# Queries and keys as seven tokens per partition, loads on one queue, and FFN pairs of one weight, in a fused attention and FFN kernel

## Chip, cores and metric

The kernel runs on one core of one Trainium2 chip. The metric is the device time in microseconds (us). Before the change it is 394.41 us, the median of three runs (393.36 to 396.3). A profiled execution is a single run; its span, 390.3 us before the change, is about 1.7 us shorter than the time of that same run, 392.04 us.

## The reference, cut to what matters

```python
q, k, v: (8 batches, 12 heads, 448 tokens, 64)
def rmsnorm(x, g):
    return x / np.sqrt(np.mean(x * x, axis=-1, keepdims=True) + 1e-06) * g
scores = np.matmul(rmsnorm(q, g_q), rmsnorm(k, g_k).transpose(0, 1, 3, 2)) / 8
attn = softmax(scores)
x = (attn @ v).transpose(0, 2, 1, 3).reshape(3584, 768)
a, b = x @ w1, x @ w2                  # 768 -> 1024 each
out = (a * b @ w3) @ w_out             # 1024 -> 1024 -> 768
```

## The kernel before

Four heads of a batch are a "quad": three quads a batch, 24 in all. A quad is loaded (its queries and keys as fp32), squared on ScalarE, summed on VectorE, scaled by the inverse norm, transposed, multiplied to scores on TensorE, exponentiated on ScalarE (seven exponentials of 128x896), and multiplied by the values. The first five quads are transposed on TensorE, the rest by DMA. Since nothing stands between `@ w3` and `@ w_out`, the kernel computes the "weight product" `w34 = w3 @ w_out` once, at the start, and the FFN then is two products a batch: FFN1 (w1 and w2, then a * b) and FFN2 (w34). TensorE interleaves all this. A model inside the program (durations of each instruction, which load lands when) fixes the order of instructions on every engine when the program is built.

The parts that the change touches:

```python
J = 4; NF = 3; REST = 64               # 448 = 64 * 4 + 64 * 3 tokens
qk_bufs = [const.tile([NP, 2, HQ, J, D], FP, ...) for z in range(3)]    # padded to 512
POOL_ORDER = "o0 o1 w0 w1 v0 w2 w3 w4 w5 v1 w6 w7 a0 b0 v2 a1 b1 a2 b2 v3".split()
GATES = {1: "w0", 2: "w5", 3: "b0", 4: "a2"}   # quad i is asked for when that weight has landed
# o = w_out, w = w3, a = w1, b = w2, v = values of a quad
# ...
def load_qk(i, which, z, eng, h0=0, n=HQ):      # z: the half with 4 or with 3 tokens a partition
    p0, p1, nj, t0, t1 = halves[z]
    return eng.dma_start(
        out=t_sb[p0:p1, h0 : h0 + n, 0:nj, :].rearrange("p h j d -> p h (j d)"),
        in_=src[b, HQ*m + h0 : HQ*m + h0 + n, t0:t1].rearrange("h (p j) d -> p h (j d)", j=nj))
# ...
for t_sb in qk_bufs:                            # the padding is set to zero
    nc.vector.memset(t_sb[REST:NP, :, :, NF, :], 0.0)
# quad 0 loaded in eight pieces, then
nc.gpsimd.tensor_copy(out=gate, in_=qk_bufs[0][:, 0, 2, 0, 0:1])   # weights wait for quad 0
# ...
def ffn1_pair(b, fi):                           # one tile of w1 beside one of w2
    nc.scalar.copy(out=hold["a"], in_=ps_all[:, z, 0:S])           # 128x448
    nc.vector.tensor_tensor(out=abT[bp][:, fi, ...], in0=ps_all[:, z + 1, 0:S],
                            in1=hold["a"], op=MULT)
    # both weights and all of x must have landed
```

Of the kernel before, what the change touches and what calls it, by code (L numbers as in the profile page):

```python
# [24 lines left out]
LAG = {"ACT": 0.11, "DVE": 0.09, "SP": 0.0, "POOL": 0.0}  # L25


class Job:



    def __init__(self, engine, took, key, emit, needs=(), done=None, moves=None):
        self.engine, self.took, self.key = engine, took, key
        self.emit, self.needs, self.done, self.moves = emit, needs, done, moves
# [5 lines left out]
class Planner:  # L40
# [3 lines left out]
    def __init__(self):  # L44
        self.free = {e: 0.0 for e in ("ACT", "DVE", "SP", "POOL", "PE")}
        self.jobs = []
        self.lanes = {"SP": [], "POOL": []}
        self.moving = {"SP": [], "POOL": []}
        self.now = 0.0
        self.landed = {"SP": [], "POOL": []}  # L50
        self.moved_to = 0.0
# [3 lines left out]

    def advance(self, t):

        while self.moved_to < t:
            heads = [
                q[0] for q in self.moving.values() if q and q[0][0] <= self.moved_to  # L60
            ]
# [5 lines left out]
            if not heads:  # L67
# [4 lines left out]
                + [x[1] * len(heads) for x in heads]  # L72
                + [z - self.moved_to for z in starts]
            )
            for x in heads:
                x[1] -= step / len(heads)
            self.moved_to += step
            for q in self.moving.values():
                if q and q[0][1] <= 1e-9:
                    q[0][2](self.moved_to + 0.7)  # L80
                    q.pop(0)

    def next_move(self):
        heads = [q[0] for q in self.moving.values() if q and q[0][0] <= self.moved_to]
        starts = [q[0][0] for q in self.moving.values() if q and q[0][0] > self.moved_to]
        return min(
            [self.moved_to + x[1] * len(heads) for x in heads] + starts, default=INF
        )

    def commit(self, job, start):  # L90
        end = start + job.took
        self.free[job.engine] = end
        end += LAG[job.engine]
        self.jobs.remove(job)
        job.emit()
        if job.moves is not None:
            entry = [end + 1.0, job.moves, None]
            ticket = [INF]
            self.landed[job.engine].append(ticket)

            def landed(t, job=job, ticket=ticket):
                ticket[0] = t
                if job.done:
                    job.done(t)

            entry[2] = landed
            self.moving[job.engine].append(entry)
        elif job.done:
            job.done(end)

# [4 lines left out]
    def run(self, pe_step, finished):  # L115

        stuck = 0
        while not finished() or self.jobs:
            best = None
            for e in ("ACT", "DVE", "SP", "POOL"):  # L120
                mine = []
                for job in self.jobs:
                    if job.engine != e:
# [4 lines left out]
                    if ready < INF:  # L128
                        mine.append((max(ready, self.free[e], self.now), job.key, job))
# [6 lines left out]
                if best is None or start < best[0]:  # L136
                    best = (start, job)
# [14 lines left out]
            if best and best[0] <= self.next_move():  # L152
                self.now = max(self.now, best[0])
                self.commit(best[1], best[0])
# [9 lines left out]
def kernel(  # L164
# [16 lines left out]
    NP = 128  # L181
    J = -(-S // NP)
    NF = S // NP
    REST = S - NF * NP
    SPLIT = REST * J
# [18 lines left out]
    ffn_pool = ctx.enter_context(tc.tile_pool(name="ffn", bufs=3))  # L204
# [6 lines left out]
    WARM = 16  # L211
    POOL_ORDER = (
        "o0 o1 w0 w1 v0 w2 w3 w4 w5 v1 w6 w7 a0 b0 v2 a1 b1 a2 b2 v3".split()
    )
    GATES = {1: "w0", 2: "w5", 3: "b0", 4: "a2"}
# [14 lines left out]
    gate = const.tile([NP, 1], FP, name="gate")  # L230
    eps_t = const.tile([NP, 1], FP, name="eps_t")
    qk_bufs = [
        const.tile([NP, 2, HQ, J, D], FP, name="qk_sb" + str(z)) for z in range(3)
# [5 lines left out]
    halves = ((0, REST, J, 0, SPLIT), (REST, NP, NF, SPLIT, S))  # L239
# [18 lines left out]
    w_at = {"w3": [INF] * CF, "w3T": [INF] * CF, "w_out": [], "w1": [], "w2": []}  # L258
# [5 lines left out]
    sent, sent_at = {}, {}  # L264
# [9 lines left out]



    def load_qk(i, which, z, eng, h0=0, n=HQ):
        b, m = divmod(i, NQB)
        t_sb = qk_bufs[i % 3][:, which]
        src = (q, k)[which]  # L280
        p0, p1, nj, t0, t1 = halves[z]
        return eng.dma_start(  # L282
            out=t_sb[p0:p1, h0 : h0 + n, 0:nj, :].rearrange("p h j d -> p h (j d)"),
            in_=src[b, HQ * m + h0 : HQ * m + h0 + n, t0:t1].rearrange(
                "h (p j) d -> p h (j d)", j=nj
            ),
        )

    def gated(i, load):
        if i in GATES:  # L290
            tc.add_manual_dep(
                load.ins, sent[GATES[i]].ins.name, SYNC_DEP, reason="DMA engines first"
            )

    def plan_load_qk(i):
        for which in range(2):
            for z in range(2):
                def done(t, which=which):
                    parts = st[i].setdefault(("in", which), [])
                    parts.append(t)  # L300
                    if len(parts) == 2:
                        landed[i]["qk"[which]] = max(parts)

                add(
                    "SP", 0.62, QUAD * i - 30 + which, 
                    lambda which=which, z=z: gated(
                        i, load_qk(i, which, z, nc.sync)
                    ),
                    needs=[
                        lambda: qk_free[i % 3],  # L310
                        lambda: sent_at.get(GATES[i], INF) if i in GATES else 0.0,
                    ],
                    done=done,
                    moves=0.9,
                )

    def v_parts(i):
        b, m = divmod(i, NQB)
        v_sb = v_bufs[i % 4]
        src = v[b, HQ * m : HQ * (m + 1)]  # L320
        lo = src[:, 0:SPLIT].rearrange("h (p j) d -> p h j d", j=J)
        hi = src[:, SPLIT:S].rearrange("h (p j) d -> p h j d", j=NF)
        return (
            (v_sb[0:REST, 0:2], lo[:, 0:2]),
            (v_sb[0:REST, 2:4, 0:NF], lo[:, 2:4, 0:NF]),
            (v_sb[REST:NP, :, 0:NF], hi),
            (v_sb[REST:NP, 2:4, NF], lo[:, 2:4, NF]),
        )

    def load_v(i, z):  # L330
        dst, part = v_parts(i)[z]
        if z < 3:
            dst = dst.rearrange("p h j d -> p h (j d)")
            part = part.rearrange("p h j d -> p h (j d)")
        nc.gpsimd.dma_start(out=dst, in_=part)  # L335

    def plan_load_v(i, key):
# [7 lines left out]
        for z in range(4):  # L345
# [3 lines left out]
                moves=(0.48, 0.39, 0.78, 0.2)[z],  # L349
# [22 lines left out]
    def plan_prep(i):  # L372
# [3 lines left out]
        sq_at, red_at = [[], []], [INF, INF]  # L376
        src = qk_bufs[i % 3]
        got = lambda w: lambda: landed[i]["qk"[w]]

        def sq(pr, parts):  # L380
            hs = slice(2 * pr, 2 * pr + 2)
            if ("sq", pr) not in s:
                s["sq", pr] = prep_pool.tile([NP, 2, 2, J, D], FP, tag="sq", name="sq")
            for t in parts:
                nc.scalar.activation(  # L385
                    out=s["sq", pr][:, t], in_=src[:, t, hs], func=AF.Square
                )

        def red(pr, parts):
            hs = slice(2 * pr, 2 * pr + 2)  # L390
            if "ssq" not in s:
                s["ssq"] = prep_pool.tile([NP, 2, HQ, J], FP, tag="ssq", name="ssq")
            nc.vector.tensor_reduce(  # L393
                out=s["ssq"][:, parts, hs, :], in_=s["sq", pr][:, parts], axis=AX, op=ADD
            )

        def alpha(h0, h1):
            if "alpha" not in s:
                s["lnv"] = prep_pool.tile([NP, 2, HQ, J], FP, tag="lnv", name="lnv")
                s["alpha"] = prep_pool.tile([NP, 2, HQ, J], FP, tag="alpha", name="al")  # L400
            lnv = s["lnv"][:, :, h0:h1]
            nc.scalar.activation(
                out=lnv, in_=s["ssq"][:, :, h0:h1], func=AF.Ln, bias=eps_t
            )
            nc.scalar.activation(  # L405
                out=s["alpha"][:, :, h0:h1], in_=lnv, func=AF.Exp, scale=-0.5
            )

        def scale(pr, parts, with_g):
            hs = slice(2 * pr, 2 * pr + 2)  # L410
            if "qkT" not in s:
                s["qkT"] = qkT_pool.tile(
                    [128, 2, 2, J * NP], BF, tag="qkT", name="qkT"
                )
            if ("qks", pr) not in s:
                s["qks", pr] = prep_pool.tile(
                    [NP, 2, J, 2, D], BF, tag="qks", name="qks"
                )
            qks = s["qks", pr]
            for t in parts:  # L420
                nc.vector.tensor_tensor(  # L421
                    out=qks[:, t].transpose([0, 2, 1, 3]),
                    in0=src[:, t, hs],
                    in1=s["alpha"][:, t, hs].unsqueeze(3).broadcast_to([NP, 2, J, D]),
                    op=MULT,
                )
            if with_g:
                nc.vector.tensor_tensor(
                    out=qks[:, 0],
                    in0=qks[:, 0],  # L430
                    in1=g_b.unsqueeze(1).unsqueeze(1).broadcast_to([NP, J, 2, D]),
                    op=MULT,
# [696 lines left out]
```

## Time and profile before

| | before |
|---|---|
| median of the timed runs | 394.41 us |
| span of the profiled run | 390.3 us |
| TensorE, ScalarE, VectorE, GpSimd busy | 94, 67, 60, 17% |
| FFN starts (first w1 pass) | 72.4 us |
| attention ends on TensorE | 298.7 us |
| mean granted TensorE clock | 0.980 |

The prediction shows the page, the chain, the stretches and the groups. One finer cut matters for what follows. This is the table of stretches, with the columns time, busy time of PE, PEld, DVE, ACT and POOL with instruction counts, granted clock, DMA share and GB/s:

```profile
12.00:20.00 8.00, 5.21 (x45) 2.39 (x46) 2.13 (x5) 5.14 (x7) 2.07 (x5) 0.71 1.15 210
20.00:72.40 52.40, 45.41 (x835) 28.51 (x835) 28.53 (x44) 28.96 (x48) 15.69 (x27) 0.94 1.00 200
```

The reader should see that TensorE is busy for only 5.21 of the 8 us from 12 to 20 us, and at a clock of 0.71.

In all that follows, "lost" is the time of a stretch less the counted work of TensorE in it: passes of 448 columns at 0.189 us, of 384 columns at 0.162 us, transposes at 0.067 us. The first two come from the chain, as the prediction works out; the last is the program's own figure (the chain of after has 0.50 us for seven, 0.071 each). PE's busy time is more than that work: over the whole run before has 365.3 us of it, and 336 us of work by the prediction's count. Up to the FFN's start before loses 11.7 us (0 to 12), 5.5 (12 to 20) and 14.2 (20 to 72.4), 31.4 together.

### The profile page before, as it was taken

Reading aid. Unit: us, or ns where it says so; the run is one execution under the profiler, and the core shown is the slowest. Engines: PE = TensorE matmul, PEld = TensorE weight load, DVE = VectorE, ACT = ScalarE, POOL = GpSimd, SP = SyncE. Lnnn points to the kernel's source line nnn. Section 1 sums busy time; section 2 is a strip of 40 time slices with the busy share of each in tenths; the row PEclk is TensorE's granted clock in tenths of the full one; section 3 lists DMA queues with packets and bytes.
Section 4 is the critical chain, followed back from the end, with each engine's and each line's share of the span. In section 5 each row is a group of like instructions: output and inputs, shape, how many; then the busy total and the mean of one; then the engine's idle time right before and its main releaser. Section 6 shows DMA issues by size and latency. Waiting matters only on the chain.

```text
span 390.3 us, 16420 instructions
## 1 busy us (share of the span) xinstructions
PE 365.3 (94%) x7361; PEld 234.5 (60%) x7361; DVE 234.9 (60%) x366; ACT 262.0 (67%) x435; POOL 68.2 (17%) x119
## 2 busy tenths in 40 slices
PE   6587996999889999999999999999999999999994
PEld 2255653555555556856566565655656778778763
DVE  5425656379786895986879778878633223323232
ACT  4515768685999999999999899999973121120210
POOL 2452231340212122222221321220000000000000
PEclk9689999899999999999999999999999999999999
DMA  4999994935999999999999999995411302302105
GB/s 97 197 223 238 219 232 89 215 40 110 167 245 179 203 180 207 195 218 163 198 161 202 202 178 188 212 236 106 64 24 47 79 2 65 104 3 81 45 12 154
DMA packets 90986, 56.38 MB, mean 144 GB/s; under 512 B 56740, under 2 KB 85668, under 8 KB 90916
## 3 DMA queue, kind: packets, MB, share of 16 engines
q1 hardware_dynamic: 70208, 42.35, 52.9%
q0 software_dynamic: 19968, 12.33, 23.8%
q8 instruction: 57, 0.93, 1.0%
q10 hardware_dynamic: 740, 0.66, 0.7%
q14 instruction: 13, 0.11, 0.1%
HBM read 46.66 MB, written 11.01 MB: 148 GB/s over the span
## 4 chain that ended last, share of the span: by engine, by line
PE 77%; DMA 11%; ACT 6%; issue 2%; SPq 1%; DVE 1%; POOL 1%; DVEq 0%; POOLq 0%; ACTq 0%
PE ps_all L709 56%; PE ps_all L624 13%; PE ps_all L577 8%; DMA qk_sb<-in_q_dram 7%; ACT P L597 3%; DMA w3s<-in_moe_w_dram 3%; DMA w2s<-in_moe_w_dram 2%; ACT sq L385 1%; PE ps_all L912 1%; SPq L282 1%; ACT Pr L597 1%; POOL w_outs L365 0%; DVE o_sb L834 0%; ACT w34s L760 0%; ACT r L639 0%
## 5 line engine op out<-in xcount | busy, mean ns | idle before, releaser
L709 PE MATMUL ps_all<-xT,w2s 64*64 64x448 bf16 x1536 | 161.6, 350 | 1.3 <-POOLq L694 0.7
L709 PE MATMUL ps_all<-xT,w1s 64*64 64x448 bf16 x1536 | 161.5, 350 | 0.0
L597 ACT ACTIVATE P<-ps_all 128x896 bf16<-128x896 f32 x144 | 126.7, 924 | 15.7 <-PE ps_all L577 15.0
L709 PEld LDWEIGHTS <-w2s 64*64 64x64 bf16 x1536 | 88.2, 107 | 28.5 <-POOLq L694 8.2
L709 PEld LDWEIGHTS <-w1s 64*64 64x64 bf16 x1536 | 89.5, 107 | 21.7 <-issue 1.2
L335 POOL DMA_DIRECT2D v_sb<-in_v_dram x96 | 58.1, 616 | 165.8 <-PE ps_all L624 142.0
L709 PE MATMUL ps_all<-w34s,abT 64*64 64x384 bf16 x1792 | 82.0, 323 | 1.7 <-ACT P L597 1.3
L786 ACT CAST a_sb<-ps_all 128x448 bf16<-128x448 f32 x64 | 34.2, 535 | 67.8 <-PE ps_all L709 67.5
L796 DVE TENSOR_TENSOR abT<-ps_all,a_sb 128x448 bf16<-128x448 f32 x64 | 39.8, 623 | 63.6 <-ACT a_sb L786 63.4
L709 PEld LDWEIGHTS <-abT 64*64 64x64 bf16 x1792 | 58.7, 107 | 18.3 <-issue 2.5
L421 DVE TENSOR_TENSOR qks<-qk_sb,al 128x512 bf16<-128x512 f32 x96 | 61.8, 685 | 11.3 <-ACT al L405 11.2
L393 DVE TENSOR_REDUCE ssq<-sq 128x16 f32<-128x1024 f32 x48 | 57.5, 1211 | 14.1 <-ACT sq L385 14.1
L385 ACT ACTIVATE sq<-qk_sb 128x512 f32<-128x512 f32 x96 | 58.1, 639 | 10.1 <-DMA qk_sb<-in_q_dram 10.0
L577 PE MATMUL ps_all<-qkT 64*64 64x448 bf16 x672 | 59.8, 361 | 2.3 <-ACT P L597 1.9
L834 DVE COPY o_sb<-ps_all 128x768 f32<-128x768 f32 (+1 forms) x29 | 26.8, 928 | 28.4 <-PE ps_all L709 28.2
L577 PEld LDWEIGHTS <-qkT 64*64 64x64 bf16 x672 | 23.3, 107 | 22.1 <-issue 14.3
L624 PE MATMUL ps_all<-P,v_sb 128*32 128x448 bf16 x576 | 36.5, 358 | 0.0
L664 DVE TENSOR_TENSOR xT<-ps_all,r 128x448 bf16<-128x448 f32 x48 | 27.7, 617 | 13.7 <-ACT r L645 12.8
L624 PEld LDWEIGHTS <-v_sb 128*32 128x32 bf16 x768 | 21.1, 98 | 16.0 <-issue 0.7
L709 PE MATMUL ps_all<-w_outs,w3T 64*64 64x384 bf16 x512 | 24.2, 330 | 0.2 <-ACT w34s L760 0.2
L624 PE MATMUL ps_all<-P,ones 128*32 128x448 bf16 x288 | 18.0, 356 | 6.1 <-ACT Pr L597 3.2
L597 ACT ACTIVATE Pr<-ps_all 128x896 bf16<-128x896 f32 x24 | 22.4, 933 | 0.0
(42 smaller groups left out, 178.5 us busy)
## 6 DMA issues: line engine op xcount, KB each, us to landing
out_dram<-o_sb SPq DMA_DIRECT2D x54, 192.0 KB, 3.5
qk_sb<-in_q_dram SPq DMA_DIRECT2D x23, 256.0 KB, 5.2
qk_sb<-in_k_dram SPq DMA_DIRECT2D x23, 256.0 KB, 5.5
qk_sb<-in_q_dram SPq DMA_DIRECT2D x23, 192.0 KB, 5.6
qk_sb<-in_k_dram SPq DMA_DIRECT2D x23, 192.0 KB, 5.7
v_sb<-in_v_dram POOLq DMA_DIRECT2D x24, 96.0 KB, 5.1
w3s<-in_moe_w_dram POOLq DMA_DIRECT2D x8, 256.0 KB, 8.0
w_outs<-in_moe_w_out_dram POOLq DMA_DIRECT2D x2, 768.0 KB, 8.4
```

Source lines behind the costliest of these rows:

```text
L335: nc.gpsimd.dma_start(out=dst, in_=part)
L385: nc.scalar.activation(out=s["sq", pr][:, t], in_=src[:, t, hs], func=AF.Square)
L393: nc.vector.tensor_reduce(out=s["ssq"][:, parts, hs, :], in_=s["sq", pr][:, parts], axis=AX, op=ADD)
L421: nc.vector.tensor_tensor(out=qks[:, t].transpose([0, 2, 1, 3]), in0=src[:, t, hs], in1=s["alpha"][:, t, hs].unsqueeze(3).broadcast_to([NP ...
L577: nc.tensor.matmul(out=sc[64 * c : 64 * c + 64, u, 0:S], lhsT=qkT[u * D : (u + 1) * D, pr, 1, k0 : k0 + 64], rhs=qkT[u * D : (u + 1) * D, ...
L597: lambda: nc.scalar.activation(out=dst, in_=sc[:, :, 0:S], func=AF.Exp),
L624: nc.tensor.matmul(out=ps[hd * HALF : (hd + 1) * HALF, :], lhsT=w, rhs=s["P"][:, hd, j, :] if j < NF else s["Pr"][:, hd % 2, :], start=(j ...
L664: lambda: nc.vector.tensor_tensor(out=xT[b][:, 2 * m + kind - 1, :], in0=ps, in1=s["r"], op=MULT),
L709: mm = nc.tensor.matmul(out=ps_all[64 * h : 64 * h + 64, p.bank + z, 0 : p.n], lhsT=lhsT[64 * r : 64 * r + 64, 64 * h : 64 * h + 64], rhs= ...
L786: nc.scalar.copy(out=hold["a"], in_=ps_all[:, z, 0:S])
L796: nc.vector.tensor_tensor(out=abT[bp][:, fi, odd * S : (odd + 1) * S], in0=ps_all[:, z + 1, 0:S], in1=hold["a"], op=MULT,)
L834: nc.vector.tensor_copy(out=hold["o"][:, n0:n1], in_=ps_all[:, z + n0 : z + n1, 0:NH])
```

## The change

The intent has four parts. Queries and keys lie as seven consecutive tokens per partition on 64 partitions a head (two heads side by side), so 448 needs no padding and each load moves runs of 7 x 64 x 4 = 1,792 bytes. The early quads' loads go into the same software queue as the weights, at chosen places, without gates. An FFN1 pair is two tiles of one weight. And the order model is revised: it has finer costs of transfers, may put some copies on ScalarE or VectorE, whichever is free, and may let a pair begin when the piece of a weight that its next pass reads has landed, where before all of it had to. (Two pairs may be open at once, before and after.) The values follow the same order of tokens, the clearing of their padding moves from VectorE to GpSimd, and the start has 20 warm-up matmuls instead of 16.

```diff
-    POOL_ORDER = (
-        "o0 o1 w0 w1 v0 w2 w3 w4 w5 v1 w6 w7 a0 b0 v2 a1 b1 a2 b2 v3".split()
-    )
-    GATES = {1: "w0", 2: "w5", 3: "b0", 4: "a2"}
+    POOL_ORDER = "w0 w1 o0 o1 w2 q1 v0 w3 w4 q2 w5 v1 w6 w7 v2 a0 a1 a2 q3 b0 b1 b2 v3 q4".split()
+    ON_POOL = (1, 2, 3, 4)
 # ... (line broken differently in the file)
-    def load_qk(i, which, z, eng, h0=0, n=HQ):
+    def load_qk(i, which, eng, x0=0, x1=2):
         return eng.dma_start(
+            out=qk_bufs[i % 3][:, which, x0:x1].rearrange("p x j d -> p x (j d)"),
+            in_=src.rearrange("(x g) (p j) d -> (g p) x (j d)", x=2, j=NJ)[:, x0:x1],
 # ...
-        for x in range(2):
-            for j in range(J):
-                nc.tensor.transpose(ps[:, x * S + j * NP : ...], s["qks", pr][0:n, x, j], ...)
+        for j in range(NJ):
+            nc.tensor.transpose(
+                ps[:, j], s["qks"][:, w, j].rearrange("p x d -> p (x d)"), ident
+            )
 # ...
-    def ffn1_pair(b, fi):
+    def ffn1_pair(b, w, f0):
+            return max(all_of(x_at[b], CM), w_at[("w1", "w2")[w]][pos // 2]) + SEM
 # ...
+        every = [(w, f0) for f0 in range(0, CF, 2) for w in range(2)]
+        waiting.extend(ffn1_pair(b, *x) for x in (sorted(every) if b == 0 else every))
 # ...
-        for t_sb in qk_bufs:
-            nc.vector.memset(t_sb[REST:NP, :, :, NF, :], 0.0)
-        nc.gpsimd.tensor_copy(out=gate, in_=qk_bufs[0][:, 0, 2, 0, 0:1])
```

## The prediction

> **What bounds the kernel now.** I read the page first (engine shares, then the forty slices), then the chain that ended last in order of time, then a table of stretches that I cut where the chain changes its nature, and last the groups. The page:
>
> ```profile
> PE 365.3 (94%) x7361; PEld 234.5 (60%) x7361; DVE 234.9 (60%) x366; ACT 262.0 (67%) x435; POOL 68.2 (17%) x119
> ...
> PEclk9689999899999999999999999999999999999999
> DMA  4999994935999999999999999995411302302105
> GB/s 97 197 223 238 219 232 89 215 40 110 167 245 179 203 180 207 195 218 163 198 161 202 202 178 188 212 236 106 64 24 47 79 2 65 104 3 81 45 12 154
> ```
>
> TensorE is "94% busy", but a busy matrix engine is not one at its peak, so the number alone does not say what can be won. The slices show a start-up of some 70 us in which the DMA engines are full from 10 to 60 us, then nearly idle from 60 to 68 us (the 89 GB/s slice and the low digit). The chain says what waited for what there:
>
> ```profile
> 3.13 3.92 DMA qk_sb<-in_q_dram
> 7.72 1.62 POOL w_outs L365 x2
> 9.33 10.32 DMA w3s<-in_moe_w_dram
> ...
> 20.31 9.54 DMA qk_sb<-in_q_dram
> ...
> 36.33 7.37 DMA w2s<-in_moe_w_dram
> ...
> 44.48 12.65 DMA qk_sb<-in_q_dram
> ...
> 66.36 3.53 PE ps_all L624 x48
> ...
> 298.66 73.68 PE ps_all L709 x1624
> ```
>
> The reader should see: nothing of the weights is issued before quad 0 is on chip (7.7 us); quad 1's queries are asked for at 20.3 us, when the weight that gates them has landed, and quad 2's at 44.5 us, when another one has. Quad 2 therefore lands at 57.1 us, its last matrix products (line 624) start at 66.4 us, and only then is the first batch's input to the FFN complete. From 117 us on the chain is TensorE almost alone, and the last 86 us are pure FFN.
>
> To see how much TensorE could give back I count its work. A "pass" is four quarter-array matmuls side by side; the chain has "2.27" us for 48 matmuls of 448 columns, so 0.189 us a pass, and 384 columns are 0.162 us by proportion. Counted from the groups in the stretches:
>
> ```profile
> 0.00:12.00 12.00, 6.70 (x21) 2.50 (x21) 7.51 (x22) 4.63 (x9) 5.17 (x14) 0.90 0.56 108
> 12.00:72.60 60.60, 50.82 (x879) 30.91 (x880) 30.82 (x49) 34.30 (x54) 17.76 (x31) 0.91 1.01 201
> 72.60:125.00 52.40, 49.55 (x980) 29.93 (x977) 38.16 (x57) 45.75 (x80) 11.47 (x19) 1.00 0.84 154
> 125.00:212.00 87.00, 86.75 (x1820) 54.58 (x1820) 70.99 (x110) 85.79 (x144) 19.88 (x33) 1.00 1.18 195
> ```
>
> (Columns: PE, PEld, DVE, ACT, POOL busy, granted clock, DMA share, GB/s.) 0 to 72.6 us holds 128 passes of the weight product, 24 of scores, 36 of attention times values, and transposes (about 9 us by the planner's own 0.075 and 0.066 us each): 20.7 + 4.5 + 6.8 + 9.0 = 41 us of work, so 31.5 us lost. 72.6 to 125 us: 45.5 us of work, 6.9 lost. 125 to 212: 83.0, 4.0 lost. 212 to 298.6: 81.5, 5.1 lost. 298.6 to 385: 84.9, 1.5 lost. Then a tail of 5.3 us. Sum: 336 of work and 54 lost, which is the span of 390.3. More than half of all that can be lost is lost before the FFN starts.
>
> [...] (DMA share 1.0 over 12 to 72.6 us). So putting quads 1 to 4 on the software queue adds no bandwidth; what it buys is order without gates. [...] 0.50 granted from 8 to 16 us, 0.60 at 20 to 24 us. The new start has the same danger.
>
> **The change part by part.**
>
> ```profile
> L335 POOL DMA_DIRECT2D v_sb<-in_v_dram x96 | 58.1, 616 | 165.8 <-PE ps_all L624 142.0
> L786 ACT CAST a_sb<-ps_all 128x448 bf16<-128x448 f32 x64 | 34.2, 535 | 67.8 <-PE ps_all L709 67.5
> L796 DVE TENSOR_TENSOR abT<-ps_all,a_sb 128x448 bf16<-128x448 f32 x64 | 39.8, 623 | 63.6 <-ACT a_sb L786 63.4
> L421 DVE TENSOR_TENSOR qks<-qk_sb,al 128x512 bf16<-128x512 f32 x96 | 61.8, 685 | 11.3 <-ACT al L405 11.2
> L393 DVE TENSOR_REDUCE ssq<-sq 128x16 f32<-128x1024 f32 x48 | 57.5, 1211 | 14.1 <-ACT sq L385 14.1
> L385 ACT ACTIVATE sq<-qk_sb 128x512 f32<-128x512 f32 x96 | 58.1, 639 | 10.1 <-DMA qk_sb<-in_q_dram 10.0
> ```
>
> *Seven tokens per partition.* The padding to 512 goes. Squares: two of 896 a quad for four of 512. Back to back an 896-wide activation costs 0.82 and a 512-wide one 0.57 (the chain and timeline), so 1.64 for 2.3: 0.6 us x 24 = 15 us of ScalarE. VectorE: reductions 24 x 2 x (1.21 - 1.07) = 7 us, scalings 96 x (0.685 - 0.624) = 6 us, gains one for two, 3 us. Transposes on TensorE: seven for eight, some 1.3 us over ten turns. DMA issues of queries and keys: 2 a quad for 4. ScalarE and VectorE are beside the path after 117 us, so on the path this is worth 1 us there; on each quad's preparation in the start-up about 1 us, against which the scores now need queries and keys of all four heads instead of one pair.
>
> *FFN pairs of one weight.* ScalarE: 32 copies of 896 (0.92) for 64 of 535 ns, 34 to 29 us. VectorE: 32 x 1.09 = 35 for 40 us. No pass is removed. Its use is in the first batch: all w1 pairs run first, and need w1 alone. Worth about 9 us of slack (4 pairs x 12 passes x 0.189) for w2, not time by itself.
>
> *Order of loads.* The weights start at about 3 us rather than 7.7. On-chip bytes that must land before the FFN's first w1 pass: w3 2.10 + w_out 1.57 + w1 1.57 + quads 1 and 2 1.83 + three values 0.69 = 7.8 MB; at the 220 GB/s of the slices from 10 to 58 us 35 us, so 40 us, to 44 with quad 5 beside it. w3's last chunk comes after 6.0 MB, 32 us; quad 2 before it, so its products are possible near 42 us. Now TensorE itself is the limit: from about 11.5 us it has 20.7 + 4.0 + 6.8 + 7 = 38.6 us of work to do before the FFN, so it begins near 51 us, not 72.6. Lost there: 51 - 38.6 = 12.5, and 1 us for the cold clock: 13.5 in place of 31.5.
>
> *After it.* Batch 0's FFN (96 + 48 passes, 26 us) and batch 1's attention on TensorE (11 us) cover the time to about 88 us; ScalarE, at some 10 us a quad, has quads 3 to 5 done by 81 to 85 if quad 4 lands by 61 us (11.4 MB). So the hole of 72.6 to 125 us shrinks to the usual 5%: all losses after the FFN's start go from 17.5 to about 14.
>
> Sum: work 336 - 1.3 = 334.7; + 13.5 + 14 + tail 5.5 (a last product of 1.09 us for 0.62) = 367.7 us of span; timed runs stand 4.1 us above it (394.41 against 390.3): 371.8. I add 1 for stalls where a new order model first errs: 373.
>
> **Rivals.** (1) *The start-up stays DMA-bound.* For it: DMA share is over 1 there, bytes don't change, and the quads now stand between the weights in one queue. Against: the gates' hole at 60 to 68 us and the late start are order, not bandwidth. If the FFN starts only at 60 us, the time is 382. (2) *Attention starves the FFN after its early start*: ScalarE is 98% busy from 125 to 212 us (85.79 of 87), and if quads 3 and 4, last in the software queue, land late, the 20 us won at the start come back as holes at 60 to 120 us; 380 to 388. Against: ScalarE loses 15 + 5 us of work. (3) *GpSimd becomes the wait*: it issues eight more loads amid the weights and also hands the pairs' halves over; loads that fill its queue make TensorE wait at the hand-over. Today TensorE's weight loads waited 10.9 us in all for it. Doubling that in the start-up gives 378 to 380. (4) *Everything better than thought*, with less lost per values product (half a microsecond per quad today, unchanged by the diff): 363.
>
> **Range and chances.** The start's gain of 18 us may be 8 to 23, and what follows -4 to +5: 364 to 385 holds 8 in 10. Within 2% of 394.4 ends at 386.5, which needs rival 1 or 2 in full: 0.09. Slower would need a mis-ordered queue: 0.02.
>
> **What would show it.** Right: the first w1 pass near 51 us (if ScalarE's or DMA's wait stands before it, that step was wrong), no low DMA digit before 60 us, quad 2 landed by 32 us, w3's last chunk by 35 us, the pure-FFN end still some 86 us or longer because attention ends earlier. Wrong: holes in TensorE between 60 and 110 us with waits for exponentials (rival 2), or waits for GpSimd's queue in the weight product (rival 3); quarter passes above 0.19 us for scores, whose moving operand is now read in runs of 64.

## The result, and the profile after

After takes 382.01 us (median of four runs, 381.49 to 385.38) against 394.21 us (four runs) of before on the same chip: a ratio of 0.9701, with a 95% interval of 0.9633 to 0.9769. A ratio here and below is the mean time of one kernel's fast runs over that of the other's fast runs of the same rounds, so it isn't quite the ratio of the quoted medians. All runs, timed and profiled, are of the fast state (none is over 1.5% above the fastest of its kernel in its call). The span of the profiled run is 380.0 us.

The page of after:

```profile
PE 360.9 (95%) x7355; PEld 245.8 (65%) x7355; DVE 214.7 (57%) x303; ACT 254.8 (67%) x359; POOL 73.9 (19%) x130
...
PEclk9689999999999999999999999999999999999999
DMA  8989999569999899996799839986005003203106
GB/s 194 254 179 126 205 285 284 69 121 193 236 184 212 226 176 219 195 184 146 147 174 275 172 51 242 225 143 69 3 2 129 2 3 98 73 3 94 36 13 156
```

The first slice now moves 194 GB/s instead of 97, so the weights do start early (the first is asked for at 2.26 us, in before at 7.72). The low digit at 60 to 68 us is gone (the next one, with 69 GB/s at 66.5 to 76 us, comes after the FFN's start), but there is a new hole at 28.5 to 38 us (126 GB/s). The chain of after, in order of time:

```profile
1.19 5.84 PE ps_all L1066 x20
7.34 2.19 DVE ssq L398 x4
...
51.51 4.66 PE ps_all L735 x108
...
102.49 9.58 DMA qkT<-qks
...
291.39 71.19 PE ps_all L735 x1552
362.67 1.10 DVE abT L818
363.82 10.62 PE ps_all L735 x256
```

No DMA piece stands in the long pieces of the start any more. It begins with 20 warm-up matmuls, then the sums of squares of quad 0, then VectorE's and TensorE's work on it. From 77 to 112 us it runs mostly through attention's exponentials and preparation on ScalarE and VectorE, and at its end through a transpose by DMA. Near the end a 1.10 us product on VectorE cuts the pure-FFN end, which before did not have such a cut. The stretches:

```profile
12.00:20.00 8.00, 5.22 (x56) 2.44 (x54) 1.55 (x3) 3.66 (x4) 1.17 (x2) 0.65 1.17 264
20.00:58.90 38.90, 38.84 (x774) 26.14 (x773) 23.90 (x35) 29.99 (x42) 17.29 (x29) 0.96 0.95 199
```

The FFN starts at 58.9 us. From 20 us to there TensorE is busy for 38.84 of 38.90 us. From 12 to 20 us TensorE is no better off than before: 5.22 of 8 us busy, at 0.65 of the clock.

The groups that answer to those of before:

```profile
L836 ACT CAST a_sb<-ps_all 128x896 bf16<-128x896 f32 x32 | 28.9, 906 | 61.9 <-PE ps_all L735 61.9
L818 DVE TENSOR_TENSOR abT<-ps_all,a_sb 128x896 bf16<-128x896 f32 x32 | 34.9, 1090 | 59.4 <-PE ps_all L735 58.3
L398 DVE TENSOR_REDUCE ssq<-sq 128x14 f32<-128x896 f32 (+1 forms) x50 | 51.1, 1042 | 18.8 <-ACT sq L391 18.7
L391 ACT ACTIVATE sq<-qk_sb 128x896 f32<-128x896 f32 (+1 forms) x50 | 45.3, 923 | 0.7 <-DMA qk_sb<-in_q_dram 0.7
```

Copies of a fall from 34.2 to 28.9 us, products from 39.8 to 34.9, reductions from 57.5 to 51.1, squares from 58.1 to 45.3. The prediction had 29, 35, 7 less and 15 less; the squares lost 12.8, the rest came out nearly as worked out. The 1.09 us that the prediction gives a product of 896 columns was its author's estimate; the trace has 1,090 ns, against 623 for 448. (Its 1.07 us for a reduction of 896 columns was an estimate too; the 46 of that size took 1,080 ns, those of 1,024 columns in before 1,211.)

The account of lost time, for all kernels of this study (us, from one profiled run each; rows with e are the experiments below):

| kernel | median | ratio, 95% | span | FFN start | lost before it | start to 125 | 125 to 212 | 212 to attention's end | to TensorE's end | tail |
|---|---|---|---|---|---|---|---|---|---|---|
| before | 394.21 | 1 | 390.3 | 72.4 | 31.4 | 7.1 | 4.0 | 5.2 | 1.1 | 5.8 |
| after | 382.01 | 0.9701, 0.9633–0.9769 | 380.0 | 58.9 | 20.0 | 6.6 | 5.4 | 5.2 | 2.1 | 5.6 |
| e1 | 383.61 | 0.9749, 0.9688–0.9810 | 382.1 | 56.7 | 17.1 | 9.9 | 7.8 | 4.4 | 2.5 | 5.5 |
| e2 | 383.42 | 0.9755, 0.9702–0.9808 | 381.4 | 59.9 | 21.3 | 6.1 | 5.5 | 5.8 | 2.1 | 5.7 |
| e3 | 380.38 | 0.9696, 0.9622–0.9770 | 376.9 | 57.4 | 18.6 | 6.4 | 6.3 | 3.9 | 1.1 | 5.6 |
| e4 | 387.65 | 0.9848, 0.9796–0.9901 | 385.5 | 65.6 | 25.9 | 5.9 | 7.1 | 3.6 | 2.5 | 5.4 |
| e5 | 381.53 | 0.9659, 0.9608–0.9710 | 379.1 | 62.9 | 22.1 | 4.6 | 6.3 | 3.5 | 2.2 | 5.6 |
| e6 | 377.74 | 0.9581, 0.9536–0.9627 | 375.2 | 58.3 | 16.9 | 4.1 | 7.1 | 3.9 | 2.1 | 5.6 |
| e7 | 385.26 | 0.9763, 0.9724–0.9803 | 384.4 | 66.9 | 27.8 | 5.5 | 4.8 | 5.5 | 0.6 | 5.5 |
| e8 | 382.93 | 0.9693, 0.9647–0.9739 | 379.0 | 57.8 | 19.2 | 5.8 | 5.9 | 6.9 | 0.7 | 5.6 |
| e9 | 379.53 | 0.9581, 0.9522–0.9640 | 378.2 | 60.1 | 19.1 | 6.1 | 7.4 | 3.9 | 1.1 | 5.6 |
| e10 | 378.63 | 0.9570, 0.9513–0.9627 | 378.9 | 61.4 | 20.2 | 4.0 | 7.9 | 4.1 | 2.1 | 5.6 |
| e11 | 376.61 | 0.9514, 0.9462–0.9567 | 373.6 | 58.7 | 17.5 | 4.1 | 6.5 | 3.9 | 0.7 | 5.6 |
| e12 | 387.25 | 0.9833, 0.9777–0.9888 | 385.2 | 66.3 | 26.8 | 5.3 | 6.7 | 5.3 | 0.6 | 5.4 |

From before to after the span falls by 10.3 us: 11.4 less lost before the FFN's start, 0.2 less tail, some 0.6 less work, and 1.9 us more lost after the start (17.4 to 19.3). One kernel's runs differ by up to 1.3%, and a stretch's figure comes from one execution. After and e8 differ by their edit only in the last batch, and yet lose 20.0 and 19.2, 6.6 and 5.8, 5.2 and 6.9 us in the same stretches. So differences of less than about 1 us in the table (2 us in the stretch after 212 us) carry nothing. The same kernel of before had a median of 393.51 us in the call of e1 to e4, 394.58 us for e5 to e8, 396.31 us for e9 to e11 and 395.1 us for e12, which is why the ratios, not the medians, are compared across calls.

### The profile page after: what moved, and what is told of

The parts are those of the page before. It is cut to its first block, busy times and chain, and to the rows that moved or that the text cites. A ratio compares the mean times of both kernels' runs of the same rounds, so it can differ in the third digit from the quotient of the medians.

```text
span 380.0 us, 16185 instructions
## 1 busy us (share of the span) xinstructions
PE 360.9 (95%) x7355; PEld 245.8 (65%) x7355; DVE 214.7 (57%) x303; ACT 254.8 (67%) x359; POOL 73.9 (19%) x130
## 3 DMA queue, kind: packets, MB, share of 16 engines
q1 hardware_dynamic: 50368, 37.43, 43.4%
## 4 chain that ended last, share of the span: by engine, by line
PE 82%; ACT 8%; DVE 4%; DMA 3%; issue 1%; DVEq 0%; POOLq 0%
PE ps_all L735 59%; PE ps_all L646 11%; PE ps_all L597 8%; ACT P L619 5%; DMA qkT<-qks 3%; DVE qks L421 2%; ACT sq L391 2%; PE ps_all L1066 2%; PE ps_all L948 1%; DVE ssq L398 1%; PE ps_all L970 1%; DVE abT L818 1%; ACT Pr L619 0%; ACT qkT L306 0%; DVE o_sb L873 0%
## 5 line engine op out<-in xcount | busy, mean ns | idle before, releaser
L735 PE MATMUL ps_all<-xT,w2s 64*64 64x448 bf16 x1536 | 89.3, 350 | 0.4
L735 PE MATMUL ps_all<-xT,w1s 64*64 64x448 bf16 x1536 | 88.0, 349 | 0.1
L735 PE MATMUL ps_all<-w34s,abT 64*64 64x384 bf16 x1792 | 83.6, 323 | 1.8 <-DVE abT L818 1.3
L735 PEld LDWEIGHTS <-abT 64*64 64x64 bf16 x1792 | 63.9, 107 | 14.8 <-issue 4.0
L836 ACT CAST a_sb<-ps_all 128x896 bf16<-128x896 f32 x32 | 28.9, 906 | 61.9 <-PE ps_all L735 61.9
L818 DVE TENSOR_TENSOR abT<-ps_all,a_sb 128x896 bf16<-128x896 f32 x32 | 34.9, 1090 | 59.4 <-PE ps_all L735 58.3
L735 PEld LDWEIGHTS <-w2s 64*64 64x64 bf16 x1536 | 53.2, 107 | 20.8 <-issue 2.3
L735 PEld LDWEIGHTS <-w1s 64*64 64x64 bf16 x1536 | 52.4, 107 | 20.5 <-POOLq L720 1.0
L421 DVE TENSOR_TENSOR qks<-qk_sb,al 128x448 bf16<-128x448 f32 x96 | 56.2, 618 | 10.0 <-ACT al L410 9.9
L398 DVE TENSOR_REDUCE ssq<-sq 128x14 f32<-128x896 f32 (+1 forms) x50 | 51.1, 1042 | 18.8 <-ACT sq L391 18.7
L873 DVE COPY o_sb<-ps_all 128x768 f32<-128x768 f32 (+1 forms) x29 | 26.8, 929 | 38.8 <-PE ps_all L735 38.5
L391 ACT ACTIVATE sq<-qk_sb 128x896 f32<-128x896 f32 (+1 forms) x50 | 45.3, 923 | 0.7 <-DMA qk_sb<-in_q_dram 0.7
L646 PEld LDWEIGHTS <-v_sb 128*32 128x32 bf16 x768 | 21.3, 97 | 15.4 <-issue 0.5
L735 PE MATMUL ps_all<-w_outs,w3T 64*64 64x384 bf16 x512 | 27.4, 349 | 0.0
L619 ACT ACTIVATE Pr<-ps_all 128x896 bf16<-128x896 f32 x24 | 22.1, 920 | 2.8 <-PE ps_all L597 2.6
L735 PEld LDWEIGHTS <-w3T 64*64 64x64 bf16 x512 | 17.9, 114 | 6.0 <-issue 1.3
```

The source lines that it names most:

```text
L391: nc.scalar.activation(out=s["sq", t][:, x0:x1], in_=src[:, t, x0:x1], func=AF.Square)
L398: nc.vector.tensor_reduce(out=s["ssq"][:, t, x0:x1], in_=s["sq", t][:, x0:x1], axis=AX, op=ADD)
L421: nc.vector.tensor_tensor(out=s["qks"][:, t, :, x], in0=src[:, t, x], in1=s["alpha"][:, t, x].unsqueeze(2).broadcast_to([NP, NJ, D]), op=MULT,
L619: lambda: nc.scalar.activation(out=dst, in_=sc[:, :, 0:S], func=AF.Exp),
L646: nc.tensor.matmul(out=ps[hd * HALF : (hd + 1) * HALF, :], lhsT=w, rhs=s["P"][:, hd, j, :] if j < NF else s["Pr"][:, hd // 2, :], start=(j ...
L735: mm = nc.tensor.matmul(out=ps_all[64 * h : 64 * h + 64, p.bank + z, 0 : p.n], lhsT=lhsT[64 * r : 64 * r + 64, 64 * h : 64 * h + 64], rhs= ...
```

## The experiments

Every kernel gave correct results. Two questions lead: which part of the change made the gain, and why the FFN starts at 58.9 and not near 51 us.

**e1: the gains' product later.** The small chain that multiplies the two gain vectors and spreads them over the partitions stands on VectorE ahead of quad 0's reductions. The timeline of after:

```profile
5.73 0.21 DVE L1070 SCALAR_TENSOR_TENSOR gp_row<-g_row 1x64 bf16<-1x64 f32 x1 [4.10 <-DMA g_row<-in_g_k_dram]
...
7.20 0.23 DVE L1077 CAST g_b<-ps_all 128x64 bf16<-128x64 f32 x1 [1.25 <-PE ps_all L1074]
7.34 2.19 DVE L398 TENSOR_REDUCE ssq<-sq 128x7 f32<-128x448 f32 x4
```

Its copy waits 1.25 us for a matmul, which starts at 6.96 us, as the 20 warm-up matmuls end (1.19 + 5.84 us), while the first square is done at 4.74 us and the other three at 6.60. The reductions stand behind that copy on VectorE, and start 0.14 us after it did.

```diff
-        nc.vector.scalar_tensor_tensor(out=gp_row, in0=g_row[:, 0], scalar=8.0, ...)
-        nc.tensor.matmul(out=ps_all[:, 6, 0:D], lhsT=ones_row, rhs=gp_row, ...)
-        nc.vector.tensor_copy(out=g_b, in_=ps_all[:, 6, 0:D])
+        def gains():  # the same three instructions
+        add("DVE", 0.9, -1000.0, gains, needs=[lambda: max(st[0]["red_at"])], done=gains_done)
```

> The product of the two gain vectors moves from ahead of quad 0's reductions to behind them; nothing else changes. Theory A (the gains, which wait for the twenty warm-up matmuls, hold VectorE's first reduction back from 4.9 to 7.3 us, and this delays everything in the start-up): the first reduction starts near 5.0 us, the first score near 12.5 us instead of 14.7, and the time falls by 1.5 to 2.5 us from the changed kernel's 382.0. Rival B (the weights' landing, w_out at 20 us, sets the start-up anyway): the first score is earlier but the time stays within 0.7 us.

```profile
4.63 0.62 DVE L398 TENSOR_REDUCE ssq<-sq 128x7 f32<-128x448 f32 x1 [3.00 <-ACT sq L391]
```

The first reduction starts at 4.63 us, and the time lost before the FFN's start falls from 20.0 to 17.1 us. The total does not fall (0.9749 against 0.9701, within the intervals): the stretches from the start to 212 us lose 17.7 us instead of 12.0. The longest sum of TensorE's waits from 55 to 212 us (columns: total us, times, longest), in after and then in e1:

```profile
PE ps_all L597 <- ACT P L619: 1.7, 3, 0.7
```

```profile
PE ps_all L597 <- ACT P L619: 3.9, 7, 0.9
```

Scores wait longer for the exponentials, as in the prediction's rival 2. All of TensorE's listed waits together grow from 3.9 to 6.3 us; the rest of the 5.7 us has no wait to its name. So that attention is the whole cause is not shown by this run (e6 tests it). Nor is e1 one change only: the order model also asked for the loads sooner (the first of w1 at 30.1 us, quad 3 at 35.4; in after 36.8 and 39.9).

The 3 us are not firm either. e6, e9, e10 and e11 carry the same edit and lose 16.9, 19.1, 20.2 and 17.5 us before the FFN, so the gain is 0 to 3 us. In the second fortieth of the span (from about 9.4 to 19 us) the pages of four of the five kernels have a granted clock of 0.8 to 1.0, and e10's, which lost most, has 0.6 to 0.7. From 12 to 20 us a matmul of 384 columns took 386 to 421 ns in the four and 524 in e10.

**e2: hand-over on SyncE.** GpSimd's queue also hands a pair's banks from one row half to the other, and these instructions wait for TensorE: in after the queue waited 4.50 us for the passes of L735 before w3's load at 21.64 us, and 1.07 us before quad 2's at 23.25. If that holds the loads behind it, then moving it elsewhere should help.

```diff
-        e = min(("POOL", "DVE", "ACT"), key=lambda e: max(free[e], at) + 0.5 * (e != "POOL"))
+        first = "SP" if t < 45.0 else "POOL"
+        e = min((first, "DVE", "ACT"), key=lambda e: max(free[e], at) + 0.5 * (e != first))
```

> Until 45 us of planned time the instruction that hands a pair's banks from one half to the other runs in SyncE's queue instead of GpSimd's. Theory A (these instructions wait for TensorE in GpSimd's queue and hold the loads behind them back; the DMA hole of 126 to 179 GB/s at 19 to 38 us is their doing, and quads 3 and 4 come late for it): the hole fills to over 220 GB/s, w1 and quad 3 are issued 4 us or more earlier, and the time falls by 2 to 4 us. Rival B (TensorE's own work up to the FFN sets its start, 58.9 us, and quads 3 and 4 are early enough): loads come earlier, the FFN starts within 1 us of 58.9 and the time stays within 1 us of 382.

```profile
GB/s 197 254 248 187 269 152 223 45 122 162 278 226 179 231 160 215 215 167 148 146 192 243 184 53 247 226 128 71 7 2 127 2 3 95 75 3 93 36 11 157
```

The hole is filled: the third and fourth slices move 248 and 187 GB/s instead of 179 and 126 (the sixth falls to 152 from 285). Quad 2 is asked for at 18.6 us instead of 23.3, the first of w1 at 29.7 instead of 36.8, quad 3 at 32.2 instead of 39.9. Yet the FFN starts at 59.9 us and the time is 0.9755. The hand-over did hold loads back, and it was not what set the time.

**e3: pairs of both weights again.** The rest as in after.

```diff
-    def ffn1_pair(b, w, f0):
+    def ffn1_pair(b, fi):                       # as in the kernel before
-        waiting.extend(ffn1_pair(b, *x) for x in (sorted(every) if b == 0 else every))
+        waiting.extend(ffn1_pair(b, fi) for fi in range(CF))
```

> The FFN pairs are again one tile of each weight, evacuated by a 448-wide copy and a 448-wide product; the rest of the change stays. Theory A (pairs of one weight hardly matter for the time): 382 within 1.5 us, with the FFN's first pass still near 59 us. Theory B (the pairs of one weight cost something: the 1.09 us product holds two banks and stands before the last FFN passes, and the losses after the FFN's start rose to 19.7 us from 17.5): 379 to 380.5. Theory C (w2 comes too late without the slack): the first passes wait for w2 and the time is 384 to 387.

It takes 380.38 us, ratio 0.9696 beside after's 0.9701. The one-weight pairs gain nothing that shows here. They do cost something at the end: the stretch from the end of attention to TensorE's end loses 1.1 us with pairs of both weights and 2.1 with pairs of one.

**e4: the old order of loads.** Layout and pairs as in after; order, gates, quads on SyncE's queue, and weights behind quad 0 as before.

```diff
-    POOL_ORDER = "w0 w1 o0 o1 w2 q1 v0 w3 w4 q2 w5 v1 w6 w7 v2 a0 a1 a2 q3 b0 b1 b2 v3 q4".split()
+    POOL_ORDER = "o0 o1 w0 w1 v0 w2 w3 w4 w5 v1 w6 w7 a0 b0 v2 a1 b1 a2 b2 v3".split()
+    ON_POOL = (); GATES = {1: "w0", 2: "w5", 3: "b0", 4: "a2"}
+        nc.gpsimd.tensor_copy(out=gate, in_=qk_bufs[0][:, 0, 1, 0, 0:1])
```

> The loads go in the old order: quads 1 to 4 on SyncE's queue behind the old gates, the weights on the software queue behind quad 0. Layout and FFN pairs stay changed. Theory A (the order is the larger part of the gain): the FFN's first pass comes at 66 to 72 us and the time is 388 to 393. Theory B (the layout, with less work on ScalarE, VectorE and DMA, is the larger part): 382 to 386.

The ratio is 0.9848: beside pairs of one weight the order is worth the difference to 0.9701, some 1.5% or 6 us, a third of the 18 us that the prediction gave it. Beside pairs of both weights (e3 against e7, below) it is 0.7% or 2.6 us, 0.9696 against 0.9763 with overlapping intervals. So the order's worth lies between nothing that shows and 6 us, depending on the pairs. The FFN starts at 65.6 us, 6.7 later than after's and still 6.8 earlier than before's, so something other than the order made the first part of that.

**e5: quad 3 earlier in the queue.** In after ScalarE goes idle while the FFN begins:

```profile
52.37 1.78 ACT L391 ACTIVATE sq<-qk_sb 128x896 f32<-128x896 f32 x2
56.19 0.80 ACT L306 CAST w34s<-ps_all 128x768 bf16<-128x768 f32 x1 [2.05 <-PE ps_all L735]
...
63.26 0.92 ACT L619 ACTIVATE P<-ps_all 128x896 bf16<-128x896 f32 x1 [4.75 <-PE ps_all L597]
```

The squares of quad 3 stand behind the last exponential of quad 2, and from their end to the first exponential of quad 3 nine us pass. At 98 to 104 us TensorE then has gaps (4.48 of 6 us busy), with the second batch's input not complete.

```diff
-"... w5 v1 w6 w7 v2 a0 a1 a2 q3 b0 b1 b2 v3 q4"
+"... w5 v1 q3 w6 w7 v2 a0 a1 a2 q4 b0 v3 b1 b2"
```

> The changed kernel with quads 3 and 4 earlier in the software queue (quad 3 before w3's last two chunks, quad 4 before w2), nothing else. Theory A (after the FFN's early start attention is what TensorE waits for: ScalarE stands idle for some 9 us between 53 and 63 us because quad 3 comes late, and TensorE pays for it near 98 to 104 us, when batch 0's FFN is done and batch 1 is not ready): quad 3's first exponential comes at 53 to 56 us instead of 63.3, the loss between the FFN's start and 125 us falls from 6.6 to about 4, and the time falls by 2 to 4 us from 382. Rival B (the weights' place in the queue is worth as much): the FFN starts 2 us or more later and the time stays within 1 us.

Quad 3's exponentials begin at about 57 us, and the loss from the start to 125 us falls from 6.6 to 4.6 us. But the FFN starts at 62.9 us, 4 us later. Of these, 2.1 us are lost (22.1 for 20.0); the other 1.9 us are work on quad 3 that TensorE now does before the FFN (start less loss: 40.8 us of work for 38.9). The date of the FFN's start alone doesn't measure a gain. The ratio, 0.9659, can't be told from after's.

**e6: e1 and a milder e5 together.** Quad 3 stands between w6 and w7.

```diff
-"... w5 v1 w6 w7 v2 a0 a1 a2 q3 b0 b1 b2 v3 q4"
+"... w5 v1 w6 q3 w7 v2 a0 a1 a2 q4 b0 v3 b1 b2"
+# and e1's edit
```

> Gains behind the reductions as in e1_gains_late, together with quad 3 before w3's last chunk and quad 4 before w2. e1_gains_late started the FFN 2.2 us earlier and lost 5.7 us more between then and 212 us. Theory A (given back because attention could not follow): with quad 3 early the start's gain stays, FFN start near 57 us, loss up to 212 us back to 12 us or less, time 377 to 379.5. Rival B (a different order of instructions gave it back, not attention's lateness): 381 to 384 again.

```profile
52.56 0.95 ACT L391 ACTIVATE sq<-qk_sb 128x896 f32<-128x896 f32 x1
53.41 1.73 ACT L619 ACTIVATE P<-ps_all 128x896 bf16<-128x896 f32 x2
```

The ratio is 0.9581, and its interval (up to 0.9627) lies below after's (from 0.9633). ScalarE is now without a gap here: the squares of quad 3 stand among quad 2's exponentials. 16.9 us are lost before the FFN's start, as in e1, and 4.1 from there to 125 us. This fits the reading that e1's gain was handed back while the next batch's attention came too late. Neither e1 nor e5 alone gave anything that the times can tell from zero; together, with quad 3 one place later than in e5, they gave 1.2%. That milder place without e1's edit was not run, so it stays open whether it alone would have done, and with it whether e1's part is needed.

**e7: the layout alone.** Old order, old pairs; the layout and the new order model stay (with the finer readiness of pairs and the 20 warm-up matmuls).

```diff
+# e3's and e4's edits together
```

> Old order of loads and old FFN pairs (e3_both_weights and e4_old_order together): the layout of queries and keys and the new order model are all that is left of the change. Theory A (parts add up: e4_old_order is 1.5% under the kernel before, and e3_both_weights gains a little on the changed kernel): 386 to 388, so the layout is worth 6 to 7 us. Theory B (the pairs of one weight do belong to the gain where w1 comes before w2): 389 to 392.

The ratio is 0.9763, about 9 us less than before, which is far more than the prediction's 1 us on the path and about 1 us for a quad's preparation. The FFN starts at 66.9 us. In the stretch from 20 to 60 us, before and then e7:

```profile
20.00:60.00 40.00, 36.73 (x711) 23.73 (x709) 20.23 (x32) 21.43 (x36) 13.29 (x23) 0.96 1.16 230
```

```profile
20.00:60.00 40.00, 38.41 (x756) 25.78 (x756) 23.15 (x33) 24.83 (x35) 15.89 (x28) 0.95 1.12 254
```

TensorE is busy for 38.41 us instead of 36.73 and the DMA engines move 254 GB/s instead of 230. (The two profiled spans differ by 5.9 us only, as before's is of one of its faster runs.) Also, the loads of quad 0 land earlier and the first weight is asked for at 5.57 us instead of 7.72. And e4, which is e7 with one-weight pairs, is slower than e7 (0.9848 against 0.9763): with the old order these pairs cost some 3 us by the ratios, whose intervals just touch, and the end of the FFN shows 1.9 of it (2.5 against 0.6).

**e8: FFN2 of the last batch begins when each tile is ready.** In after the last FFN2 pairs need all of the last batch's a * b, so TensorE stands still for the last 1.10 us product (1.3 us by the list of waits).

```diff
-                need.append(all_of(ab_at[2 * bp + bb], CF // 2))
+                got = ab_at[2 * bp + bb]
+                need.append((got[pos // 2] if len(got) > pos // 2 else INF) if 2 * bp + bb >= 7
+                            else all_of(got, CF // 2))
```

> In the last batch the second FFN product may begin as soon as the first tiles of its input are there, instead of after all eight; the 1.1 us product of VectorE before it (TensorE stood idle 1.3 us for it at 362.7 us) is then hidden. Theory A: 1 to 1.5 us less than the changed kernel, 380.5 to 381. Rival B (the end hides it behind another wait, such as a bank): within 0.5 us of 382.

```profile
291.82 81.59 PE ps_all L735 x1808
```

The chain has one unbroken piece where after has three, and the stretch loses 0.7 instead of 2.1 us. The times don't resolve it: 0.9693 beside 0.9701 (the stretch before it lost 6.9 us for 5.2).

**e9: e6 with pairs of both weights.**

```diff
+# e6's and e3's edits together
```

> e6_gains_q3 with the FFN pairs of both weights again. Theory A (parts add up: pairs of one weight cost some 1.5 us in e3_both_weights): 375.5 to 376.5. Rival B (what e3_both_weights gained came from its start, 57.4 us against 58.9, which e6_gains_q3 has already): 377 to 379.

The ratio is 0.9581, the same as e6's. So the way of pairing is worth nothing that the times can tell once attention keeps up (the intervals are 1% wide).

**e10: e6 with the hand-over on SyncE.**

```diff
+# e6's and e2's edits together
```

> e6_gains_q3 with the hand-over instruction on SyncE's queue until 45 us of planned time. In e2_handover_sp the loads came up to 8 us earlier and the time did not fall. Theory A (loads' landing is not what the FFN's start or attention wait for, so GpSimd's queue is harmless here): the same as e6_gains_q3 within 1 us, 377 to 378.7. Theory B (the DMA hole hurts once the start is quicker): 1.5 us or more faster, under 376.2.

The ratio is 0.9570, the same as e6's. But this is a weak test: in e6 the loads are early already (quad 2 asked for at 19.9 us, the first of w1 at 33.7), and here they are hardly earlier (20.6 and 32.0). It says nothing of what earlier loads would give; e2 alone tests that.

**e11: e6 with e8's end.**

```diff
+# e6's and e8's edits together
```

> e6_gains_q3 with the last batch's second FFN product started per tile as in e8_ffn2_tail, where the last stretch lost 0.7 us instead of 2.1 but the whole was no faster. Theory A (the 1.4 us are real and e8_ffn2_tail lost them in another order elsewhere): 376 to 377. Rival B (no gain): 377.5 to 378.5.

It takes 376.61 us (375.51 to 376.71), ratio 0.9514 (0.9462 to 0.9567): the fastest kernel of the study, below before and, by intervals that don't touch, below after. The end's 1.4 us are seen again (0.7 lost in that stretch against e6's 2.1).

**e12: e7 with the loads in two pieces.** Is it the longer run of bytes that makes e7's gain?

```diff
+        for j0, j1 in ((0, J), (J, NJ)):       # 4 and 3 tokens: 1,024 and 768 bytes
+            got = eng.dma_start(
+                out=qk_bufs[i % 3][:, which, x0:x1, j0:j1].rearrange("p x j d -> p x (j d)"),
+                in_=src[:, x0:x1, j0:j1].rearrange("p x j d -> p x (j d)"))
```

> The layout-alone kernel (new layout, old order, old pairs; 385.26 in its call, ratio 0.9763), with one thing undone: each load of a quad's queries or keys is again two, of four and of three tokens per partition, so that a packet is 1,024 or 768 bytes instead of 1,792 and a quad has four issues instead of two. The compute side is as in the layout-alone kernel. Theory A (the layout's 9 us come mostly from the transfers of a start that DMA bounds: longer packets, fewer issues): the bytes moved from 20 to 60 us fall back from 235 to 290 towards the 220 to 235 GB/s of the kernel before, the FFN starts 2 to 5 us later than 66.9, and the time is 388 to 391, ratio 0.985 to 0.99. Rival B (they come from the shorter work on ScalarE and VectorE, the fewer transposes and the new order model): the time is within 1.5 us of the layout-alone kernel, ratio 0.974 to 0.980, and the FFN starts at 66 to 68 us.

```profile
20.00:60.00 40.00, 38.37 (x749) 25.82 (x747) 23.35 (x33) 23.49 (x33) 16.25 (x28) 0.94 1.13 248
```

The time, 387.25 us (ratio 0.9833), falls between the two expectations, and the two intervals (0.9724 to 0.9803 for e7, 0.9777 to 0.9888 here) overlap a little. The difference of the ratios is 0.7% (2.8 us), and the intervals allow anything from nothing to some 5 us. So by the estimate two thirds of the 9 us are there without long runs; that it is more than half is likely and not shown. Theory A's mechanism did not show: the rate is 248 GB/s against 254 and not back at 230, and the FFN starts at 66.3 us, not later. The packets of the hardware queue took 179.5 us of 16 engines' time here (46.6% of 385.2 us) and 169.5 in e7 (44.1% of 384.4), 5.6% less with the long runs; but the same queue took 164.9 us in after and 152.8 in e1, with 50,368 packets each, and it carries outputs and transposes too. So what the longer runs save there is not settled. Here, too, the first weight is asked for early, at 5.89 us, with the same eight load pieces of quad 0 as before. The four of SyncE's queue took 1.84 us to issue, in before 3.00. What the layout removed there are the three memsets of padding on VectorE, which ran until 3.37 us in before; the trace names no wait of the issues for them, so that they were the cause is likely and not shown.

## Why the prediction was right or wrong

The direction, faster by over 2%, and the range, 364 to 385 us, held, in part by luck: the order of loads, which was to bring 18 us, brings some 6 at most, and the layout with the new order model, which was to bring a few, brings 9 (e4, e7). The point of 373.0 us was 9 us too low. By its own sum the span was to be 367.7 us and is 380.0, so 12.3 us are missing (the extra that it added for timed runs, 4.1 + 1 us, was in fact 2.0, which hides 3 of them: the 4.1 set the median of the timed runs against the span of a faster one, whose own time was 392.04).

**The bound that it named.** The prediction read the chain's loads at 20.3 and 44.5 us as quads 1 and 2 and concluded that quad 2 lands at 57.1 us and holds the FFN back. That is off by one quad. A quad has four squares; quad 1's four are at 29.9 to 33.8 us, and the next ones on ScalarE in the kernel before are:

```profile
41.74 1.15 ACT L385 ACTIVATE sq<-qk_sb 128x512 f32<-128x512 f32 x2
...
46.03 1.14 ACT L385 ACTIVATE sq<-qk_sb 128x512 f32<-128x512 f32 x2
...
57.21 0.63 ACT L385 ACTIVATE sq<-qk_sb 128x512 f32<-128x512 f32 x1 [0.70 <-DMA qk_sb<-in_q_dram]
```

The first four of these are quad 2, on chip by 41.7 us; the load that landed at 57.1 us is quad 3 (the gates say the same: quad 3 waits for "b0", the first of w2). The chain passed through quad 3 only because its squares stand among quad 2's exponentials on ScalarE. The gap on ScalarE for this load was 0.70 us. So the load of quad 2 was not the wait whose removal brings the FFN forward. e2, in which quads 2 and 3 are asked for 5 and 8 us sooner without any gain, agrees.

**"Lost there: 13.5 in place of 31.5".** This is the term that was mis-sized most: 20.0, so 6.5 us (and 1 us of the 13.5 was counted twice: 51 us is 1 us after the 50.1 of 11.5 + 38.6 already). The finer cut of the kernel before shows the step that failed: of the 31.4 us, 17.2 are lost before 20 us and only 14.2 after. The change brought the latter down to 4.1, better than one could ask, and the former only to 15.9. For 12 to 20 us the prediction had nothing but "1 us for the cold clock", its author's estimate. The stretch lost 5.4 us: TensorE stood still for 2.8 us, 2.0 of it in waits for quad 0's exponentials, and was busy for 5.22 us, at a clock of 0.65, with 2.6 us of counted work. (Before has 5.21 us busy at 0.71 and lost 5.5, e12 5.67 at 0.50 and lost 5.3.) "From about 11.5 us it has 38.6 us of work" was right as an amount (58.9 less 20.0 is 38.9) and wrong in taking all time from 11.5 us on for work: by 20 us only some 4 us of it was done. e1 points to one cause, the gains ahead of the reductions, at 0 to 3 us. (The reading of the granted clock, 0.50 from 8 to 16 us, is also off: it is 0.60 there, and 0.50 from 10 to 16.) No kernel of the study lost less than 16.9 us before the start, so what a start of 51 us would need stays open.

**"All losses after the FFN's start go from 17.5 to about 14".** They went to 19.3, 5.3 us off. Rival 2, held to be unlikely because ScalarE loses work, came true in a small form. ScalarE's total load was not the point; one quad's place in the queues was, and with it the 9 us without an exponential on ScalarE at 54 to 63 us. The prediction had asked for quad 4 to land by 61 us and did not ask when quad 3's squares would get their turn. e6 closes this hole (4.1 against 6.6 us to 125 us) and keeps the start. Of the rest, 1.4 us is the gap ahead of the last 1.09 us product, which the prediction had put at 0.5 (1.09 for 0.62) in the tail: with pairs of one weight all of TensorE's last FFN2 passes wait for it (e8, e11). Why the stretch of 125 to 212 us loses 5.4 to 7.9 us in kernels with the new order, against 4.0 in before, stays open; the old order has 4.8 (e7), 6.7 (e12) and 7.1 (e4).

**The seven tokens.** "1 us there, about 1 us on each quad's preparation", 2 to 4 us as one reads it, was too small by a factor of two to four: e7's gain is 9 us, the order model's part in it. The savings per instruction were nearly right. That the conclusion "beside the path" failed because ScalarE and VectorE are part of each quad's path at the start is likely and not shown; what shows is that TensorE does more in the same 40 us (38.41 against 36.73 us of PE). The prediction also passed over two things that the layout removes. Each of the 38 transposes by DMA moves seven tiles for eight: 38 x 128 x 128 x 2 bytes are 1.25 MB, just what the hardware queue moves less (42.35 to 41.10 MB, before and e7). And the start has no padding of queries and keys to clear: quad 0 is there 1.7 us sooner (the copy that waits for it starts at 5.45 us in e7, at 7.19 in before). e12 puts the share of longer runs at 3 us of the nine, within 0 to 5. How the rest divides between less work, the earlier start and the new order model isn't separated, because no kernel was run with the old model and the new layout.

**The pairs of one weight.** "Slack, not time" was right as to the gain (e3 and e9 are no slower) and silent on the price, 1.0 to 1.9 us at the end (e3, e4).

**Rivals 1 and 3.** Rival 1 had the numbers (a start at 60 us gives 382) and not the cause: from 20 to 58.9 us the DMA share is 0.95 and 199 GB/s are moved (before, from 20 to 72.4 us: 1.00 and 200), TensorE is busy throughout, and earlier loads change nothing (e2). Rival 3 did not come: TensorE's weight loads waited 2.6 us for GpSimd's queue instead of 10.9. The converse did, the hand-over held loads back, and it cost nothing that the times show (e2).

**The other signs.** Quad 2's squares start at 32.5 us and w3's last chunk lands at about 36 us, near the 32 and 35 that were named, and no DMA digit is low before 60 us. A matmul of scores took 360 ns on the mean, in before 361. The pure-FFN end lasts 83 us and not "some 86 us or longer".

**The order of loads.** Right in direction. It is worth 0.7 to 1.5%, 3 to 6 us (e3 against e7, after against e4), instead of 18 us at the start, because the layout with the order model already brings the FFN's start from 72.4 to 66.9 us, and because most of the rest lies before 20 us.

**The sum of the parts.** From the ratios: layout with order model 2.4% (e7), pairs of one weight on top of it -0.9% (e4 against e7), order on top of both 1.5% (after against e4), together the 3.0% of the result. By the other way round, order first, it is 2.4%, 0.7% (e3 against e7) and 0.0% for the pairs. Both ways begin with layout and order model, which make most of the gain; what order and pairs add to it together, 0.6%, is within the intervals.

## What to carry to other kernels

Before you price a change by "lost time at the start", cut the start finely enough to see which part of the loss the change can reach, and check each piece of the chain against a count of the loop's own instructions, since one quad's load may stand on another quad's path. A remedy that gains nothing alone may do so beside another: try two together before you give one up, and run each alone in the very form in which it stands in the pair. Where two parts of a change interact, price each one beside both forms of the other. A change of layout is to be priced on the start-up path too, with everything it removes: padding to clear, tiles to transpose, not only the width of instructions.
